# The second block's second product by seven products for two pairs of token chunks instead of one

## Chip, cores and metric

One core of a Trainium2 chip runs the whole program. The metric is the device time of one execution in microseconds, as the median of three runs.

## The reference

Attention (a coarse one on means of four tokens plus a local one in a band of seven), then two blocks on 2304 tokens of 512 channels. The change touches the second block and the layer norm ahead of it. Cut to that:

```python
def _moe2_ref(x, g_ln, w_ch1, w_ch2):          # x: (4, 576, 512), float32
    mu = np.mean(x, axis=-1, keepdims=True)
    var = np.mean((x - mu) ** 2, axis=-1, keepdims=True)
    xn = (x - mu) / np.sqrt(var + 1e-06) * g_ln
    ch = np.maximum(xn @ w_ch1, 0.0) @ w_ch2    # w_ch1: 512 x 2048, w_ch2: 2048 x 512, float64 in memory
    return (x + ch).astype(np.float32)
```

## The kernel before

Every instruction but the preparations is recorded with `add(engine, cost, prio, fn, r=, w=)`: its engine or a choice of engines, a cost, a priority, what it reads and writes. `Plan.order` (lines 137 to 240) then makes the order of the work by list scheduling on these costs: of the operations that are ready it takes the one that can begin first, and of those that can begin at the same time the one with the lowest priority number. Each engine then runs its own list in that order. All DMAs are issued by one engine, SP, one after the other; an SP instruction that waits holds all DMAs behind it. Buffers come from tags with a fixed number of slots, and a buffer takes a slot when the slot's former one has been read for the last time.

Every product is in split precision: each factor is a high and a low part (`F32R`), and `mm3` (lines 791 to 794) makes three matmuls for one, high by high, high by low, low by high.

The tokens are cut into six chunks of C = 384 (three tiles of 128). The first block works chunk by chunk. The second block, from about 384 us on, works on pairs of chunks: p = 0, 1 and 2, called here the first, the middle and the last pair. With two chunks and two halves of the channels, a product is a 2 by 2 product of blocks, which a Strassen-like scheme makes with seven block products in place of eight.

In each pair, `m2_prep` loads the pair's rows (x1t), makes the layer norm, writes it to `z_dram` and reads it back in a layout from which DVE can transpose (zb, lines 1009 to 1017: 32 DMAs per pair in runs of 32 floats), multiplies by g_ln and makes differences. `m2_split` makes the seven combinations xn in high and low parts. The first product takes for each f of eight (a block of 128 columns in each half of the 2048) seven products of six matmuls of 384 columns, with the weights `sa` loaded from `s_dram`, where `w1_combine` has put their seven combinations.

The second product has two forms. For p below KEEP (line 1163), `m2_h` splits each of the four results of an f into high and low parts, and `m2_acc` multiplies them with W2 as it is: 512 columns, six token tiles, two halves. For p from KEEP on, `m2_h_keep` leaves all results q in SBUF (in the slots that W2 had), and `m2_out_keep` makes seven products again: for each product and f a combination of q is split into hh and hl and multiplied with `ta`, loaded from `t_dram`, 256 columns, three token tiles. The combinations in `t_dram` are made by `w2_combine` from W2, through tiles `raw` and `t` (tag "wa", four slots), during the pair before the first one that needs them. PRM["keep"] is 1, so KEEP is 2: the first and the middle pair have the first form, the last pair the second, and w2_combine runs in the middle pair.

The weights `sa` have seven slots, one for each product; `ta` runs through eleven slots, these seven and the four of "wa". In the first product for f = 0 and 1 all results go to the two banks of the tag "pk"; later ones have more.

W2 is loaded as float64 and converted on ACT and DVE (`load_split`, `load_f32`): four of sixteen tiles in the last chunk of the first block, twelve during the first pair.

Of the kernel before, what the change touches and what calls it, by code (L numbers as in the profile page):

```python
# [9 lines left out]
F32 = mybir.dt.float32  # L10
# [26 lines left out]
    tp=0.5, tps=0.05, keep=1, tg=-2, ne=12, we=52.842, wes=25.704, wel=6.378,  # L37
# [37 lines left out]
class Plan:  # L75
# [61 lines left out]
    def order(self):  # L137
# [27 lines left out]
        while ready:  # L165
# [114 lines left out]
def attn_moe_kernel(  # L280
# [634 lines left out]

    def w1_convert(fo, d, prio):
        w1_early.add((fo, d))
        f = Buf(wk, [P, 512], F32, "wf", 2)
        load_f32(w_ch1[d * P:(d + 1) * P, 512 * fo:512 * fo + 512], f, prio)
# [4 lines left out]
    def w1_combine(g, j, prio):  # L924
# [3 lines left out]
        for x, fo, d in w1_parts(g, j):  # L928
# [4 lines left out]
            else:  # L933
                load_f32(w_ch1[d * P:(d + 1) * P, 512 * fo:512 * fo + 512], a[x], prio)
# [32 lines left out]
    def m2_prep(p, load_prio, prio):  # L967
# [39 lines left out]
        for j in range(2):  # L1007
            b = Buf(xpool, [P, 6, C], F32, "xT", 2, f"raw{j}")
            for q, (kt, c) in enumerate(((j, 2 * p), (j, 2 * p + 1), (j + 2, 2 * p), (j + 2, 2 * p + 1))):
                zb = Buf(wk, [P, C], F32, "tmu", 2, "zb")  # L1010
                for a in range(4):
                    add("SP", c_dma(32 * C * 4, 128), prio, lambda kt=kt, a=a, zb=zb, c=c: nc.sync.dma_start(
                        out=zb()[32 * a:32 * a + 32].rearrange("p (n f) -> p n f", f=32),
                        in_=z_dram[c * C:c * C + C, P * kt + 32 * a:P * kt + 32 * a + 32].rearrange(
                            "(n p) f -> p n f", p=32)), r=[(zd, (c, t)) for t in range(TT)], w=[(zb, a)], lat=2.2)
                add("DVE", c_dve(C), prio, lambda b=b, q=q, zb=zb: nc.vector.transpose(out=b()[:, q], in_=zb()),
                    r=[zb], w=[(b, q)])
                add("ACT", c_act(C, ap=1), prio, lambda b=b, q=q, kt=kt: nc.scalar.mul(
                    b()[:, q], b()[:, q], gln[:, kt:kt + 1]), r=[glb], w=[(b, q)])
# [4 lines left out]
            raws.append((b, s))  # L1024
# [3 lines left out]
    HL = "hl"  # L1028

    def b_place(p, i, j, x):  # L1030
        if p == 1 and i == 1:
            return w1tiles, f"alt{2 * j + x}", None
        if p == 1 and i == 6:
# [129 lines left out]
    KEEP = 3 - PRM["keep"]  # L1163

    def w2_combine(f, prio, after):
# [10 lines left out]
        raw = [Buf(w1tiles, [P, 512], F32, f"alt{2 * (f % 2) + k}", 1, "t") if KEEP == 1 else  # L1176
# [358 lines left out]
```

## Time and profile before

| | us |
|---|---|
| median of three runs | 765.13 (764.07 to 766.21) |
| the profiled execution | 766.57 |
| its span, first to last instruction | 764.8 |
| PE busy | 747.9 (98%) |
| DVE busy | 583.0 (76%) |
| ACT busy | 437.9 (57%) |
| POOL busy | 85.9 (11%) |

The span is the time from the first to the last instruction of the profiled execution; its own time is 1.8 us longer. A busy time is the time in which at least one instruction of the engine ran. PE is TensorE, DVE VectorE, ACT ScalarE, POOL GpSimd, SP the engine that issues the DMAs. Matmuls overlap: one of 384 columns is listed with some 0.34 us but the next begins 0.174 us after it, so a matmul's price is read from the distance of starts or from counts in a full stretch.

### The profile page before, as it was taken

To read this page: it belongs to the slowest core of one execution; us is meant where nothing else is said; L and a number is where in the kernel's file an instruction comes from. 1 tells how busy PE (TensorE), PEld (TensorE's weight loads), DVE (VectorE), ACT (ScalarE), POOL (GpSimd) and SP (SyncE) were. 2 spreads that over 40 slices of the span, in tenths; PEclk is the share of its full clock that TensorE was granted. 3 is DMA by queue.
4 is the path that set the end of the run, shared out by engine and by line. 5 is a ranking of instruction groups with operands and counts; after the bars stand their busy time and mean duration, and the time that the engine had idled before them with its cause. 6 is when DMAs were issued, how large, how long until landed. Compare 5 with 4: busy or idle time off the path is not lost.

```text
span 764.8 us, 16744 instructions
## 1 busy us (share of the span) xinstructions
PE 747.9 (98%) x6032; PEld 655.5 (86%) x6032; DVE 583.0 (76%) x1217; ACT 437.9 (57%) x1009; POOL 85.9 (11%) x140
## 2 busy tenths in 40 slices
PE   9999999999999999999999999999999999999998
PEld 6878777788778798888988899889887989999997
DVE  5899999998975958978989864476765776334986
ACT  5889998887785756858844541221332343343552
POOL 3011123112100000000110000020121110110101
PEclk9999999999999999999999999999999999999999
DMA  9998596877787896984778894469899986988784
GB/s 194 199 187 188 175 177 135 178 165 151 201 182 217 264 318 182 271 255 133 151 250 299 238 258 122 115 220 312 240 262 318 370 291 223 307 254 254 246 267 142
DMA packets 222623, 170.34 MB, mean 223 GB/s; under 512 B 129088, under 2 KB 168908, under 8 KB 222540
## 3 DMA queue, kind: packets, MB, share of 16 engines
q1 hardware_dynamic: 222540, 169.27, 78.6%
q8 instruction: 48, 0.79, 0.5%
q14 instruction: 35, 0.29, 0.1%
HBM read 122.56 MB, written 46.66 MB: 221 GB/s over the span
## 4 chain that ended last, share of the span: by engine, by line
PE 72%; DVE 13%; DMA 7%; ACT 4%; issue 2%; SPq 1%; POOL 0%; DVEq 0%; ACTq 0%; POOLq 0%
PE pso L793 7%; PE pso L794 7%; PE pso L792 7%; PE psh L792 7%; PE psh L793 6%; PE psh L794 6%; PE psk L792 4%; PE psv L792 4%; PE psk L794 3%; PE psk L793 3%; PE psv L793 3%; PE psv L794 3%; PE warm L447 2%; DMA w<-in_moe_w_ch_dram 2%; DMA zb<-z_dram 2%
## 5 line engine op out<-in xcount | busy, mean ns | idle before, releaser
L792 PE MATMUL psh<-xn,sa 128*128 128x384 f32 x336 | 114.1, 340 | 3.2 <-DVE c11l L1098 1.2
L793 PE MATMUL psh<-xn,sa 128*128 128x384 f32 x336 | 113.4, 338 | 0.0
L794 PE MATMUL psh<-xn,sa 128*128 128x384 f32 x336 | 113.1, 337 | 0.0
L792 PEld LDWEIGHTS psh<-xn,sa 128*128 128x128 f32 x336 | 63.1, 188 | 10.8 <-DVE c L1129 1.9
L793 PEld LDWEIGHTS psh<-xn,sa 128*128 128x128 f32 x336 | 63.1, 188 | 4.2 <-DVE xn L1066 0.2
L794 PEld LDWEIGHTS psh<-xn,sa 128*128 128x128 f32 x336 | 63.1, 188 | 0.0
L794 PE MATMUL pso<-ta,hl 128*128 128x256 f32 x168 | 47.4, 282 | 0.0
L793 PE MATMUL pso<-ta,hh 128*128 128x256 f32 x168 | 47.3, 281 | 0.0
L792 PE MATMUL pso<-ta,hh 128*128 128x256 f32 x168 | 47.1, 281 | 0.0
L389 ACT CAST hh<-q 128x384 fp32r<-128x384 f32 x55 | 28.4, 516 | 26.1 <-PE pso L793 23.9
L409 ACT ACTIVATE wf<-w 128x512 f32<-128x512 f32 x48 | 32.2, 671 | 14.8 <-DMA w<-in_moe_w_ch_dram 7.0
L416 DVE SCALAR_TENSOR_TENSOR wf<-wf,w 128x512 uint32<-128x512 uint32 x48 | 32.8, 686 | 8.9 <-ACT w L411 8.7
L393 ACT ACTIVATE kr<-psk 128x384 f32<-128x384 f32 x46 | 22.5, 489 | 24.2 <-PE psk L794 20.2
L857 DVE TENSOR_TENSOR kl<-kr,kh 128x384 fp32r<-128x384 f32 x43 | 23.8, 553 | 14.9 <-ACT kr L856 14.6
L411 ACT ACTIVATE w<-w 128x512 uint32<-128x512 uint8 x52 | 34.8, 669 | 0.0
L816 DVE SCALAR_TENSOR_TENSOR tmu<-xT,oms,tmu 128x384 f32<-128x384 f32 (+1 forms) x64 | 31.7, 512 | 2.1 <-ACT tmu L810 2.0
L420 DVE SCALAR_TENSOR_TENSOR wf<-w,wf 128x512 uint32<-128x512 uint32 x48 | 32.9, 686 | 0.3
L901 DVE TENSOR_TENSOR hl<-q,hh 128x384 fp32r<-128x384 f32 x47 | 26.0, 557 | 8.1 <-ACT hh L389 7.6
L794 PEld LDWEIGHTS pso<-ta,hl 128*128 128x128 f32 x168 | 31.7, 189 | 0.0
L792 PEld LDWEIGHTS pso<-ta,hh 128*128 128x128 f32 x168 | 31.7, 188 | 0.0
L793 PEld LDWEIGHTS pso<-ta,hh 128*128 128x128 f32 x168 | 31.6, 188 | 0.0
L810 ACT ACTIVATE tmu<-xT,vecs 128x384 f32<-128x384 f32 (+1 forms) x51 | 26.8, 538 | 6.9 <-DVE xrl L820 4.0
(573 smaller groups left out, 2178.5 us busy)
## 6 DMA issues: line engine op xcount, KB each, us to landing
sa<-s_dram SPq DMA_DIRECT2D x168, 256.0 KB, 3.7
w<-in_moe_w_ch_dram SPq DMA_DIRECT2D x32, 512.0 KB, 6.3
s_dram<-s SPq DMA_DIRECT2D x56, 256.0 KB, 4.0
ta<-t_dram SPq DMA_DIRECT2D x56, 256.0 KB, 3.1
t_dram<-t SPq DMA_DIRECT2D x32, 256.0 KB, 4.9
vw<-in_v_dram SPq DMA_DIRECT2D x62, 96.0 KB, 4.1
x_dram<-r SPq DMA_DIRECT2D x18, 256.0 KB, 3.3
x1t<-x_dram SPq DMA_DIRECT2D x6, 768.0 KB
```

What stands on the lines that cost most here:

```text
L389: return [("ACT", c_act(n), lambda: nc.scalar.copy(dst(), src()), False), ("DVE", c_dve(n, True), lambda: nc.vector.tensor_copy(dst(), src ...
L409: add("ACT", c_act(512), prio, lambda: nc.scalar.activation(f(), w64().bitcast(F32)[:, :, 1], AF.Abs, scale=2.0 ** -112), r=[w64], w=[f])
L411: add("ACT", c_act(512), prio, lambda: nc.scalar.activation(w64()[:, :, 0], w64().bitcast(U8).rearrange("p a (b c) -> p a b c", c=4)[:, :, ...
L416: lambda: nc.vector.scalar_tensor_tensor(fu(), fu(), 3, w64()[:, :, 0], op0=ALU.logical_shift_left, op1=ALU.bitwise_or),
L420: lambda: nc.vector.scalar_tensor_tensor(fu(), w64()[:, :, 1], 0x80000000, fu(), op0=ALU.bitwise_and, op1=ALU.bitwise_or),
L792: nc.tensor.matmul(ps, lh, rh, start=start, stop=False, skip_group_check=more)
L793: nc.tensor.matmul(ps, lh, rl, start=False, stop=False, skip_group_check=more)
L794: nc.tensor.matmul(ps, ll, rh, start=False, stop=stop, skip_group_check=more)
L810: add([("ACT", c_act(n, ap=1), lambda t=t, o=o, n=n, cur=cur, kt=kt: nc.scalar.mul(t()[:, o:o + n], cur(), mu[:, kt:kt + 1]), False), ("DV ...
L816: lambda t=t, o=o, n=n, prv=prv, kt=kt: nc.vector.scalar_tensor_tensor(t()[:, o:o + n], prv(), om[:, kt:kt + 1], t()[:, o:o + n], op0=ALU. ...
L857: add(either(C, lambda e: e.tensor_tensor(kl(), kr(), kh().bitcast(F32), op=ALU.subtract)), 0, prio, None, r=[kr, kh], w=[kl])
L901: add(either(n, lambda e: e.tensor_tensor(lo(), src(), hi().bitcast(F32), op=ALU.subtract)), 0, prio, None, r=r + wh, w=wl)
```

## The change

The middle pair's second product takes the second form too (keep = 2, so KEEP = 1). So `w2_combine` runs in the first pair, its operations waiting for the first pair's `m2_acc` three steps back instead of two (tg). Its tile `raw` moves to the tag "wf". For f below 6 the piece of W2 that the product i = 1 needs isn't written to `t_dram` but copied to SBUF by `w2_stay`, into the slots "xrh" and "xrl", and stays there for both pairs; so the last pair's xn of i = 1 and 6 take the places that the middle pair's have. In the pairs of the second form, `sa` and `ta` go through one ring of eleven slots. zb is read in runs of 128 floats (512 bytes) in 16 DMAs per pair, each for half a chunk and all four channel blocks, and transposed with a stride; for that the channels are permuted, which the loads of w_ch1 and g_ln follow. The planner gets a term that holds SP back after 330 us of planned time when transfers are behind.

```diff
-    tp=0.5, tps=0.05, keep=1, tg=-2, ne=12, we=52.842, wes=25.704, wel=6.378,
+    late=330.0, ahead=1.0, tp=0.5, tps=0.05, keep=2, tg=-3, b11=6, ne=12, we=52.842, wes=25.704, wel=6.378,
...
                 moved = max(moved, free[eng]) + cost
+                if at > PRM["late"]:
+                    free[eng] = max(free[eng], moved - PRM["ahead"])
                 end = moved + o.lat
...
+    def w1_rows(d, fo):
+        return w_ch1.rearrange("(p k) f -> k p f", k=KT)[d, :, 512 * fo:512 * fo + 512]
...
-            for q, (kt, c) in enumerate(((j, 2 * p), (j, 2 * p + 1), (j + 2, 2 * p), (j + 2, 2 * p + 1))):
-                zb = Buf(wk, [P, C], F32, "tmu", 2, "zb")
+            raws.append(b)
+        for c in (2 * p, 2 * p + 1):
+            for h in range(2):
+                zb = Buf(wk, [P, C // 64, P], F32, "w64", 2, "zb")
                 for a in range(4):
...
+                    row = c * C + C // 2 * h
+                    add("SP", c_dma(32 * C * 8, 512), prio, lambda a=a, zb=zb, row=row: nc.sync.dma_start(
+                        out=zb()[32 * a:32 * a + 32], in_=z_dram[row:row + C // 2, P * a:P * a + P].rearrange(
+                            "(n p) f -> p n f", p=32)), r=[(zd, (c, t)) for t in (range(2) if h == 0 else range(1, TT))],
+                        w=[(zb, a)], lat=2.2)
+                for kt in range(KT):
+                    b, q = raws[kt % 2], 2 * (kt // 2) + c % 2
+                    add("DVE", c_dve(C // 2), prio, lambda b=b, q=q, kt=kt, h=h, zb=zb: nc.vector.transpose(
+                        out=b()[:, q, C // 2 * h:C // 2 * h + C // 2], in_=zb()[:, :, kt:P:KT]),
+                        r=[zb], w=[(b, (q, h))])
...
+    KEEP = 3 - PRM["keep"]
+    N11 = PRM["b11"] if KEEP == 1 else 0
 
     def b_place(p, i, j, x):
-        if p == 1 and i == 1:
+        if (p == 1 or p == 2 and N11) and i == 1:
             return w1tiles, f"alt{2 * j + x}", None
-        if p == 1 and i == 6:
+        if (p == 1 or p == 2 and N11) and i == 6:
             return wp, f"s{16 + j}{HL[x]}", None
...
-    def m2_product(f, i, ps, xn, prio, first):
-
-        s = Buf(w1tiles, [P, 2, 2, P], F32R, f"sa{i}", 1)
+    def m2_product(f, i, ps, xn, prio, first, kept=False):
+
+        s = ring([P, 2, 2, P], "sa") if kept else Buf(w1tiles, [P, 2, 2, P], F32R, f"sa{i}", 1)
...
+    B11, stay = {}, [None]
+    n_ring = [0]
+
+    def ring(shape, name):
+        k = n_ring[0] % 11
+        n_ring[0] += 1
+        return Buf(w1tiles, shape, F32R, *((f"sa{SEQ[k]}", 1) if k < 7 else ("wa", 4)), name)
+
+    def w2_stay(f, prio):
+
+        if f % 3 == 0:
+            stay[0] = Buf(wk, [P, 3, 2, 256], F32R, f"xr{HL[f // 3]}", 1, "b11")
+        b = stay[0]
+        B11[f] = [View(b, (f % 3, x), lambda t, x=x: t[:, f % 3, x]) for x in range(2)]
+        for x in range(2):
+            add(copy(256, B11[f][x], lambda x=x: W2[f][x]()[:, :256]), 0, prio, None, r=[W2[f][x]], w=[B11[f][x]])
...
             for k, (i0, n) in enumerate(((0, 1), (1, 2))):
+                if k == 0 and f < N11:
+                    continue
...
-        raw = [Buf(w1tiles, [P, 512], F32, f"alt{2 * (f % 2) + k}", 1, "t") if KEEP == 1 else
+        raw = [Buf(wk, [P, 512], F32, "wf", 2, "t") if KEEP == 1 else
...
-                k = (F4 * n + f) % 11 if n < 6 or last else 0
-                ta = Buf(w1tiles, [P, 2, 256], F32R, *((f"sa{SEQ[k - 4]}", 1) if k > 3 else ("wa", 4)), "ta")
...
+                if i == 1 and f in B11:
+                    rh, rl = B11[f]
+                    need_ = [rh, rl]
+                else:
+                    ta = ring([P, 2, 256], "ta")
...
+            for f in range(N11):
+                w2_stay(f, T - 5 + f)
```

In `m2_h_keep` all seven calls of `m2_product` get the argument kept = True, and the load of g_ln reads "(p k) -> k p".

## Rows read from the trace of the kernel before

**Rows 1.** The page, busy time by engine: us, share of span, instructions.

```profile
PE 747.9 (98%) x6032; PEld 655.5 (86%) x6032; DVE 583.0 (76%) x1217; ACT 437.9 (57%) x1009; POOL 85.9 (11%) x140
```

**Rows 2.** Busy time by stage: stretch, length, engines (instructions), clock, DMA share, GB/s.

```profile
384.00:508.50 124.50, 123.40 (x611) 109.91 (x611) 84.41 (x167) 46.17 (x92) 10.90 (x9) 1.00 0.69 208
508.50:637.00 128.50, 126.39 (x624) 112.31 (x623) 93.30 (x198) 41.50 (x95) 18.34 (x21) 1.00 0.92 297
...
645.00:701.00 56.00, 56.00 (x316) 55.02 (x316) 21.85 (x39) 19.57 (x40) 5.10 (x5) 1.00 0.85 275
701.00:761.00 60.00, 59.99 (x506) 59.78 (x504) 52.34 (x107) 27.57 (x57) 6.62 (x6) 1.00 0.72 225
```

**Rows 3.** PE's waits, 570 to 645 us: line, releaser, us in total, times, longest.

```profile
PE psh L792 <- DVE c11l L1098: 1.2, 1, 1.2
PE psh L792 <- DVE c L1129: 0.7, 1, 0.7
PE psh L792 <- ACT u L385: 0.2, 1, 0.2
```

**Rows 4.** DVE in order of time near 577 us: start, length, instruction, idle before.

```profile
577.23 0.58 DVE L1016 STREAM_TRANSPOSE raw<-zb 128x384 f32<-128x384 f32 x1 [2.10 <-DMA zb<-z_dram]
```

**Rows 5.** PE in order of time at the end of the first pair.

```profile
507.32 0.40 PE L792 MATMUL pso<-w27h,c12h 128*128 128x512 f32 x1
...
508.72 0.34 PE L792 MATMUL psh<-xn,sa 128*128 128x384 f32 x1
```

**Rows 6.** Groups of DVE's instructions, 701 to 761 us: busy, mean ns, idle before.

```profile
L901 DVE TENSOR_TENSOR hl<-q,hh 128x384 fp32r<-128x384 f32 x46 | 25.5, 557 | 6.7 <-ACT hh L389 6.1
L905 DVE TENSOR_TENSOR q<-q,q 128x384 f32<-128x384 f32 x30 | 17.1, 578 | 0.0
```

**Rows 7.** The same, 384 to 508 us.

```profile
L1066 DVE TENSOR_TENSOR xn<-raw,xn 128x384 fp32r<-128x384 f32 x13 | 8.0, 622 | 1.9 <-ACT xn L389 1.8
```

**Rows 8.** DVE and POOL in order of time, 750 to 761 us.

```profile
752.99 1.27 DVE L1267 TENSOR_TENSOR uv<-uv 128x256 f32<-128x256 f32 x1
758.61 0.42 DVE L1267 TENSOR_TENSOR uv<-uv 128x256 f32<-128x256 f32 x1
752.96 3.33 POOL L901 TENSOR_TENSOR hl<-q,hh 128x384 fp32r<-128x384 f32 x3 [7.47 <-ACT hh L389]
```

**Rows 9.** PE in order of time at the start of the first pair.

```profile
386.78 0.39 PE L794 MATMUL psv<-wv7h,kl 128*128 128x512 f32 x1
...
389.66 0.45 PE L792 MATMUL psh<-xn,sa 128*128 128x384 f32 x1 [0.18 <-DVE u L1112]
```

**Rows 10.** Groups of DVE's instructions, 508 to 645 us; the additions L1180 by one.

```profile
L901 DVE TENSOR_TENSOR t<-t 128x256 fp32r<-128x256 f32 x25 | 10.7, 428 | 9.7 <-ACT t L389 9.6
L905 DVE TENSOR_TENSOR t<-t 128x256 f32<-128x256 f32 x21 | 8.8, 420 | 1.6 <-POOL t L905 1.3
...
L1180 DVE TENSOR_TENSOR t<-w210h,w210l 128x512 f32<-128x512 f32 x1 | 0.7, 693 | 0.1
```

**Rows 11.** The page, DMA issues: count, KB each, median us to landing.

```profile
sa<-s_dram SPq DMA_DIRECT2D x168, 256.0 KB, 3.7
...
ta<-t_dram SPq DMA_DIRECT2D x56, 256.0 KB, 3.1
...
zb<-z_dram SPq DMA_DIRECT2D x96, 48.0 KB, 3.0
```

**Rows 12.** DMA packets, MB and share of 16 engines: 510 to 570, then 570 to 645 us.

```profile
DMA packets 20290, 16.58 MB, mean 276 GB/s; under 512 B 12126, under 2 KB 13662, under 8 KB 20285
q1 hardware_dynamic: 20285, 16.52, 90.9%
DMA packets 16339, 22.72 MB, mean 303 GB/s; under 512 B 3071, under 2 KB 7679, under 8 KB 16332
q1 hardware_dynamic: 16332, 22.64, 89.0%
```

**Rows 13.** SP's issue of g_ln (ns), and of kin in order of time.

```profile
L1369 SPq DMA_DIRECT2D vraw<-in_moe_g_ln_dram x1: 293/293/293, 8.6 to 8.6; - x1
13.21 3.58 SPq L506 DMA_DIRECT2D kin<-in_k_dram  x4
```

More of the change, by code (lines that the diff above doesn't have):

```diff
@@ L918, in w1_convert @@
         f = Buf(wk, [P, 512], F32, "wf", 2)
-        load_f32(w_ch1[d * P:(d + 1) * P, 512 * fo:512 * fo + 512], f, prio)
+        load_f32(w1_rows(d, fo), f, prio)
         add("SP", c_dma(P * 2048), prio, lambda: nc.sync.dma_start(out=w1_dram[fo, d], in_=f()),
@@ L933, in w1_combine @@
             else:
-                load_f32(w_ch1[d * P:(d + 1) * P, 512 * fo:512 * fo + 512], a[x], prio)
+                load_f32(w1_rows(d, fo), a[x], prio)
         def put(i, src):
@@ L1008, in m2_prep @@
             b = Buf(xpool, [P, 6, C], F32, "xT", 2, f"raw{j}")
-            for q, (kt, c) in enumerate(((j, 2 * p), (j, 2 * p + 1), (j + 2, 2 * p), (j + 2, 2 * p + 1))):
-                zb = Buf(wk, [P, C], F32, "tmu", 2, "zb")
+            raws.append(b)
+        for c in (2 * p, 2 * p + 1):
+            for h in range(2):
+                zb = Buf(wk, [P, C // 64, P], F32, "w64", 2, "zb")
                 for a in range(4):
[L1012 to L1017, printed above, removed]
+                    row = c * C + C // 2 * h
[8 more added lines that the diff above has]
+                        r=[zb], w=[(b, (q, h))])
+        for j in range(2):
+            b = raws[j]
+            for q in range(4):
+                kt = j + 2 * (q // 2)
                 add("ACT", c_act(C, ap=1), prio, lambda b=b, q=q, kt=kt: nc.scalar.mul(
-                    b()[:, q], b()[:, q], gln[:, kt:kt + 1]), r=[glb], w=[(b, q)])
+                    b()[:, q], b()[:, q], gln[:, kt:kt + 1]), r=[glb, (b, (q, 0)), (b, (q, 1))], w=[(b, q)])
             s = lambda q, b=b: (lambda: b()[:, q])
@@ L1023, in m2_prep @@
             minus(C, s(5), s(3), s(1), prio, [(b, 3), (b, 1)], [(b, 5)])
-            raws.append((b, s))
+            raws[j] = b, s
         return raws
     HL = "hl"
+    KEEP = 3 - PRM["keep"]
+    N11 = PRM["b11"] if KEEP == 1 else 0
     def b_place(p, i, j, x):
-        if p == 1 and i == 1:
+        if (p == 1 or p == 2 and N11) and i == 1:
             return w1tiles, f"alt{2 * j + x}", None
-        if p == 1 and i == 6:
+        if (p == 1 or p == 2 and N11) and i == 6:
             return wp, f"s{16 + j}{HL[x]}", None
@@ L1162, in attn_moe_kernel @@
     acc_op = {}
-    KEEP = 3 - PRM["keep"]
+    B11, stay = {}, [None]
[11 more added lines that the diff above has]
+            add(copy(256, B11[f][x], lambda x=x: W2[f][x]()[:, :256]), 0, prio, None, r=[W2[f][x]], w=[B11[f][x]])
     def w2_combine(f, prio, after):
@@ L1309, in m2_out_keep @@
                 split(C, hh, hl, src, prio, [src], [hh], [hl])
-                k = (F4 * n + f) % 11 if n < 6 or last else 0
-                ta = Buf(w1tiles, [P, 2, 256], F32R, *((f"sa{SEQ[k - 4]}", 1) if k > 3 else ("wa", 4)), "ta")
-                add("SP", c_dma(P * 2048), prio - PRM["sld"], lambda ta=ta, f=f, i=i: nc.sync.dma_start(
-                    out=ta().bitcast(F32), in_=t_dram[f, TI[i]]),
-                    r=[(td, (TI[i], f, y)) for y in range(2)], w=[ta], lat=2.2)
-                rh, rl = (View(ta, None, lambda t, y=y: t[:, y]) for y in range(2))
-                need_ = [ta]
+                if i == 1 and f in B11:
[3 more added lines that the diff above has]
+                    ta = ring([P, 2, 256], "ta")
+                    add("SP", c_dma(P * 2048), prio - PRM["sld"], lambda ta=ta, f=f, i=i: nc.sync.dma_start(
+                        out=ta().bitcast(F32), in_=t_dram[f, TI[i]]),
+                        r=[(td, (TI[i], f, y)) for y in range(2)], w=[ta], lat=2.2)
+                    rh, rl = (View(ta, None, lambda t, y=y: t[:, y]) for y in range(2))
+                    need_ = [ta]
                 def mm(ts, f=f, hh=hh, hl=hl, rh=rh, rl=rl, cur=cur, fresh=fresh):
@@ L1369, in attn_moe_kernel @@
                 add("SP", 0.05, PRM["mu"], lambda i=i, src=src: nc.sync.dma_start(
-                    out=raw()[KT * i:KT * i + KT, :P], in_=src.rearrange("(k p) -> k p", p=P)), w=[(raw, i)], lat=2.2)
+                    out=raw()[KT * i:KT * i + KT, :P],
+                    in_=src.rearrange("(p k) -> k p" if src is g_ln else "(k p) -> k p", p=P)), w=[(raw, i)], lat=2.2)
             vps = Buf(ps_k, [P, 512], F32, "pk", 2, "vps")
```

14 lines of the change are left out of this document (7 added, 7 removed).

## The prediction

> **What bounds the kernel now.** I read the page first: PE is busy 98% of the span [rows 1], so time falls only if PE gets less to do or waits less. Then a table of busy time by stage, cut where the pairs of the second block begin and end [rows 2]. The reader is to see that from 384 us on PE is full in every stage (123.40 of 124.5, 126.39 of 128.5, 56.0 of 56.0, 59.99 of 60.0) at a granted clock of 1.00, that DVE is second (84.41, 93.30, 21.85, 52.34 us), and that the DMA share is highest in the middle pair, 0.92 at 297 GB/s. The middle pair's 128.5 us hold 2.1 us in which PE did nothing. Next the list of PE's waits in the second half of that pair [rows 3]: 1.2 + 0.7 + 0.2 = 2.1 us, all on DVE or ACT. The longest goes back to DVE's order of work: it stood 2.10 us before a transpose whose zb had not landed, and c11l, which PE wanted, was queued behind it [rows 4]. So PE bounds, and the DMA queue reaches PE through DVE.
>
> **The change part by part.** *Second product of the middle pair.* Now: 8 f by 6 token tiles by 2 halves by 3 = 288 matmuls of 512 columns. Six of them in a row begin from 507.32 until one of 384 columns begins at 508.72, so one takes 1.40 / 6 = 0.2333 us [rows 5]; 288 x 0.2333 = 67.2 us. After: 7 products by 8 f by 3 tiles by 3 = 504 of 256 columns. The last pair runs this form already: 506 matmuls in 59.99 us, 0.1186 each [rows 2]; 504 x 0.1186 = 59.8 us. All of it is on PE, and PE sets the end: **-7.4 us**. The first product, 336 matmuls of 384 columns at 56.0 / 316 = 0.177 us [rows 2], is the same in either form.
>
> *What DVE pays.* The old form's splits of c11 to c21 go (four per f), 32 q additions stay, and the out phase brings 56 subtractions hl of 0.557 us and 32 of q or pool of 0.578 us [rows 6], plus the additions into res. In the last pair this fits: DVE 52.34 and POOL 6.62 us beside 59.99 us of PE, without a wait [rows 2]. The middle pair's out phase gets something the last one has not: the split of the next pair's xn, 14 subtractions of 0.622 us [rows 7] and two more minus of 0.578, 9.9 us. 52.34 + 6.62 + 9.9 = 68.9 us against 59.8 us of PE, if DVE and POOL can't work at once: 9.1 us too much. That they hardly can, a row shows: while POOL did three hl (752.96 to 756.29), DVE's uv<-uv took 1.27 us, and 0.42 us when POOL was idle [rows 8]. Cost: 0 to +9.1 us. I take 0, since only the first two of seven xn are needed when the last pair begins, the rest up to 6 us later, and the stage after has DVE at 21.85 of 56.0 us [rows 2].
>
> The Trainium skill (SBUF — State Buffer, Who interferes with whom) says that a DVE instruction with two SBUF inputs and a GpSimd instruction that reads SBUF exclude each other for the whole instruction. The trace agrees as far as the 1.27 us goes. By that rule the out phase would be the 68.9 us, and this is the second rival below.
>
> *Hand-over to the last pair.* Before, its first steps ran between the middle pair's last 36 matmuls of 512 columns. After, nothing of that kind is left over, and steps f = 0 and 1 have two PSUM banks in the pool "pk", each waiting for an ACT or DVE instruction. The start of the first pair shows the price: between 386.78 and 389.66, 2.88 us, stand one 512-column matmul (0.23) and nine of 384 columns (0.177 each, 1.59), so 1.06 us was lost in one step [rows 9]. Two steps: 0 to 2.1 us; I take **+1.1**, since products of the out phase can fill in.
>
> *w2_combine moved by one pair.* Per f it adds two tiles of 512, makes four minus and four splits of 256, and writes 1 MB of t plus raw pieces of W2: 8 x 1792 KB = 14.7 MB, less 6 x 256 KB that are kept in SBUF, 13.1 MB. It leaves the middle pair, where the 2.1 us of waits stood, and enters the first, where it is queued on DVE, ACT and SP between the W2 loads and the sa loads. On DVE it took 10.7 + 8.8 us and sixteen additions of 0.69, 30.5 us in all [rows 10], so DVE in the first pair goes from 84.41 to some 115 of 124.5 us; the tile wf serves loads and combine in turn, and res of n = 0 and 3 after them. None of its output is wanted before the middle pair's out phase, 60 us later. So only its company costs: I move the 2.1 us with it, **0**, with -2.1 (they vanish) and +2.1 (both pairs have them) as ends.
>
> *Bytes.* One sa or ta is 256 KB [rows 11]. First pair after: 208 GB/s x 124.5 us = 25.9 MB, plus 13.1 = 39.0 MB, 313 GB/s. Middle pair after: 297 x 128.5 = 38.2 MB, less 14.7, plus 50 ta (13.1) = 36.6 MB in 119 us (128.5 - 7.4 - 2.1), 308 GB/s. Is there room? Two windows with different mixtures give the price of a packet [rows 12]: 12,126 short packets and 15.03 MB of long ones took 90.9% of 16 x 60 us, 3,071 and 22.33 MB 89.0% of 16 x 75 us; solved, 0.0153 us per 128-byte packet and 45.7 engine-us per MB, 350 GB/s at a full share. The zb loads are now 32 per pair of 384 packets [rows 11], 188 engine-us; after, 16 of 192 packets of 512 bytes, between 72 (by bytes) and 188 (four times a short one). With that the first pair comes to 111 to 119 of 124.5 us, the middle to 104 to 112 of 119 us, at most 95% and 94%. The middle pair ran at 92% with 2.1 us lost, so I take 0 here; the other end is the last rival.
>
> *Ring of 11, waits and queues.* Weights of the first product wait for 11 slots instead of their own one of seven; SP, in which sa waits for PE now, gets 11 x 1.06 = 11.7 us of lead (six matmuls of 0.177 each) against 7 x 1.06 = 7.4. Behind a waiting sa stand all other DMAs, as before. Cost 0. The 12 copies of w2_stay (256 columns, ACT, 0.4 us each) run while PE finishes the first pair's last step: 0, and if the cover is gone 12 x 0.4 = 4.8 us on ACT, half idle there.
>
> *zb in halves* makes 16 transposes of 192 instead of 8 of 384 per pair and SP issues 16 instead of 32: 0. *w_ch1 rows* keep their run length: 0. *g_ln* becomes 512 runs of 4 bytes; its row is 0.293 us of SP, and the nearest with as many packets, kin in four pieces of 576, takes 3.58 / 4 = 0.90 us [rows 13]: 0 to +0.6 early in the queue, I take **+0.3**. *The planner's new term* changes only the order on SP after its own 330 us: 0.
>
> **Sum.** -7.4 + 1.1 + 0.3 = -6.0 us. Against the profiled execution's 766.57 us (764.8 span and 1.8 around it): 760.6. That execution stood 1.44 us above the median of 765.13, so 759.1 us.
>
> **The rivals.** *All cover holds:* also the 2.1 us vanish, since zb costs fewer packets and the combine has left the pair with the most bytes, and the hand-over is free. 766.57 - 7.4 - 2.1 - 1.44 = 755.6. For it: the last pair lost nothing at all. Against: two pairs at a DMA share near 0.9 where there was one.
>
> *DVE and POOL become the bound* of the middle pair's out phase: 759.1 - 1.1 + 9.1 = 767.1, no change. For it: 1.27 against 0.42 us [rows 8]. Against: the free DVE time after it [rows 2].
>
> *Slower, the single DMA queue.* All transfers go through SP's queue in order, and the two pairs need 75.6 MB in what was 253 us. If the queue carries no more than the middle pair's 297 GB/s, they take 254.5 us: +1.5, with the hand-over and g_ln +2.9, so 768.0; at the 276 GB/s of 510 to 570 us [rows 12] it would be 274 us and 788. It decides from about 298 GB/s downward. For it: the first pair goes from 208 to 313. Against: 303 GB/s in 570 to 645 at 89% [rows 12], with less than 2.2 us lost.
>
> That the change does nothing is excluded as far as a trace can: the same code runs in the last pair at the 0.1186 us used here.
>
> **How the numbers follow.** 0.3%, or 2.3 us, is about what a measurement of this kernel can tell from no change. Chances: forecast 0.55 (own range 756.8 to 763), all cover 0.18, DVE and POOL 0.15, DMA queue 0.12. Faster (below 762.8): nine tenths of the first, the second, and a tenth of the third, 0.69. Within: 0.17. Slower (above 767.4): 0.14. The range goes from 754.6 (one us below the second case) to 766.8, which leaves part of the third and the fourth out above.
>
> **What would show it.** Right: pso of the middle pair as 504 matmuls of 256 columns near 0.1186 us; its out phase near 60 us; t_dram writes before the middle pair; waits of PE below 4 us from 384 us on. Hand-over wrong: no gap, or over 2.1 us, in the last pair's first two steps. DVE rival: hl as the releaser of pso, DVE and POOL together at the whole out phase. DMA rival: sa or ta as releasers of PE. The prediction is wrong altogether if PE shows new waits of more than 7 us.

## The result and the profile after

| | before | after |
|---|---|---|
| median | 766.31 (764.07 to 767.24, 6 runs) | 770.26 (767.09 to 773.96, 6 runs) |
| ratio | | 1.0052, 95% interval 1.0029 to 1.0074 |
| the profiled execution, its span | 766.57, 764.8 | 770.0, 767.9 |

The changed kernel is slower by 0.5%. The forecast was 759.1 us, with 766.8 as its upper bound; it was built on a median of 765.13 us for the kernel before, which six runs put at 766.31. One run below (777.16 us, of the kernel with tg = -1 and raw in "wf") was in a slower state of the clock and is left out of that kernel's figures.

The page of the changed kernel, busy time by engine, answers to [rows 1]:

```profile
PE 744.3 (97%) x6248; PEld 662.6 (86%) x6248; DVE 622.6 (81%) x1322; ACT 469.2 (61%) x1079; POOL 93.7 (12%) x143
```

PE has less to do than before, 744.3 against 747.9 us, and the span is still longer. Busy time by stage of the changed kernel, columns as in [rows 2]. The first pair now ends near 520 us, the middle pair's out phase fills the third row, and the last two rows are the last pair:

```profile
388.50:520.00 131.50, 123.02 (x588) 107.24 (x586) 109.36 (x236) 57.08 (x128) 15.58 (x17) 0.97 0.88 290
520.00:590.00 70.00, 69.05 (x397) 67.02 (x398) 53.52 (x116) 31.16 (x67) 8.57 (x8) 1.00 0.98 339
590.00:646.00 56.00, 56.00 (x471) 56.00 (x469) 53.59 (x111) 28.66 (x61) 10.09 (x8) 1.00 0.80 238
646.00:701.00 55.00, 55.00 (x320) 55.00 (x319) 20.94 (x39) 21.15 (x43) 6.07 (x6) 1.00 0.92 309
701.00:761.00 60.00, 60.00 (x498) 60.00 (x497) 50.78 (x101) 28.40 (x59) 6.62 (x6) 1.00 0.66 208
```

From 590 us on PE is full. Of the 9.4 us in which PE did nothing from 388.5 us on, 131.5 - 123.0 = 8.5 lie in the first pair, where before it was 1.1 of 124.5, and the granted clock of that stage is 0.97 instead of 1.00. PE's waits from 384 to 646 us, in the columns of [rows 3]:

```profile
PE psh L794 <- DVE c L1142: 2.9, 2, 2.2
PE pso L796 <- DVE c21l L1115: 2.8, 1, 2.8
PE pso L796 <- DVE c12l L1115: 1.5, 2, 1.2
PE psh L794 <- DMA sa<-s_dram: 1.0, 2, 0.6
PE psh L794 <- ACT u L387: 0.6, 2, 0.3
PE psh L794 <- DVE c L1146: 0.5, 1, 0.5
```

They sum to 9.3 us; the same list of the kernel before sums to 3.1:

```profile
PE psh L792 <- DVE c11l L1098: 1.2, 1, 1.2
PE psh L792 <- DVE c L1129: 0.8, 2, 0.7
PE psh L792 <- ACT u L385: 0.5, 2, 0.3
PE psh L792 <- DVE c L1125: 0.4, 1, 0.4
PE psh L792 <- DVE u L1112: 0.2, 1, 0.2
```

The longest wait of the changed kernel can be followed back through three engines. ACT, DVE and PE of the changed kernel in order of time near 487 us (start, length, instruction, idle before it and what ended that):

```profile
487.06 0.41 ACT L391 CAST t<-t 128x256 fp32r<-128x256 f32 x1 [2.44 <-DMA t_dram<-t]
...
487.50 0.43 DVE L903 TENSOR_TENSOR t<-t 128x256 fp32r<-128x256 f32 x1 [2.16 <-ACT t L391]
487.84 0.42 DVE L907 TENSOR_TENSOR t<-t 128x256 f32<-128x256 f32 x1
488.18 0.55 DVE L1115 SCALAR_TENSOR_TENSOR c21l<-c,c21h 128x384 fp32r<-128x384 f32 x1
...
485.56 0.40 PE L795 MATMUL pso<-w213l,c21h 128*128 128x512 f32 x1
488.78 0.79 PE L796 MATMUL pso<-w213h,c21l 128*128 128x512 f32 x1 [2.83 <-DVE c21l L1115]
```

A cast of `w2_combine` writes a tile t in the tag "wa", whose four slots come free when a write to `t_dram` has landed. ACT stood 2.44 us for that; DVE's next instruction, a subtraction of the combine, stood 2.16 us for ACT; and the split c21l, which PE wanted, was queued behind it. The landing that ACT waited for fell into a stretch in which the DMA engines were full (a share of 1.06 at 405 GB/s from 486 to 488 us, in the next rows), so the DMA queue has a part in this wait, though PE's list names DVE.

The wait costs more than its length. PE's starts after it are 0.32 us apart for 384 columns and 0.43 for 512, where the same matmuls before the gap started 0.177 and 0.233 apart. The granted clock is the column before the DMA share, in windows of 2 us:

```profile
486.00:488.00 2.00, 0.00 (x0) 0.00 (x0) 0.50 (x2) 0.41 (x1) 0.00 (x0) 1.00 1.06 405
488.00:490.00 2.00, 1.22 (x3) 1.04 (x4) 2.00 (x6) 0.74 (x2) 0.89 (x1) 0.55 1.00 385
490.00:492.00 2.00, 2.00 (x7) 1.90 (x7) 2.00 (x6) 0.81 (x3) 0.00 (x0) 0.50 0.42 157
492.00:494.00 2.00, 2.00 (x6) 1.52 (x6) 1.44 (x3) 0.08 (x1) 1.16 (x2) 0.50 0.44 151
494.00:496.00 2.00, 2.00 (x10) 1.77 (x9) 0.00 (x0) 0.00 (x0) 1.03 (x2) 0.74 0.97 374
496.00:498.00 2.00, 2.00 (x13) 2.00 (x12) 1.16 (x3) 0.83 (x3) 0.00 (x0) 1.00 0.31 87
```

At 0.50, which is 1.2 of 2.4 GHz, ten matmuls of 512 columns and six of 384 took the 6.33 us from 488.78 to 495.11; at full clock they are 10 x 0.233 + 6 x 0.177 = 3.4 us. So 2.9 us went into the clock.

With that the two profiled executions can be balanced: -7.4 (the new form), +6.2 (waits, 9.3 - 3.1), +2.9 (clock), and +1.7 at the start of the block, since the last matmul of 512 columns ahead of the first pair (the mark, below), at 386.78 us in [rows 9], is now at 388.47. The sum is +3.4 us; measured 770.0 - 766.57 = +3.4 (their spans differ by 3.1). That it fits so closely is luck in part: the -7.4 is worked out from counts and distances, and the mark differs by more than 1.7 us even between kernels that load g_ln alike (see below).

### The profile page after: what moved, and what is told of

Its sections match the earlier page's. It is cut to its first block, busy times and chain, and to the rows that moved or that the text cites. A ratio compares the mean times of both kernels' runs of the same rounds, so it can differ in the third digit from the quotient of the medians.

```text
span 767.9 us, 17471 instructions
## 1 busy us (share of the span) xinstructions
PE 744.3 (97%) x6248; PEld 662.6 (86%) x6248; DVE 622.6 (81%) x1322; ACT 469.2 (61%) x1079; POOL 93.7 (12%) x143
## 4 chain that ended last, share of the span: by engine, by line
PE 70%; DVE 12%; DMA 10%; ACT 5%; issue 3%; POOL 1%; SPq 0%; DVEq 0%; ACTq 0%; POOLq 0%
PE pso L796 6%; PE pso L794 6%; PE pso L795 6%; PE psh L794 6%; PE psh L795 6%; PE psh L796 6%; DMA w<-in_moe_w_ch_dram 4%; PE psk L794 4%; PE psv L794 4%; PE psv L795 4%; PE psv L796 4%; PE psk L796 3%; PE psk L795 3%; DMA sa<-s_dram 2%; PE sc L645 2%
## 5 line engine op out<-in xcount | busy, mean ns | idle before, releaser
L391 ACT CAST hh<-q 128x384 fp32r<-128x384 f32 x109 | 56.2, 516 | 48.0 <-PE pso L795 43.7
L796 PE MATMUL pso<-ta,hl 128*128 128x256 f32 x300 | 84.4, 281 | 0.0
L794 PE MATMUL pso<-ta,hh 128*128 128x256 f32 x300 | 84.3, 281 | 0.0
L795 PE MATMUL pso<-ta,hh 128*128 128x256 f32 x300 | 84.3, 281 | 0.0
L903 DVE TENSOR_TENSOR hl<-q,hh 128x384 fp32r<-128x384 f32 x92 | 51.3, 564 | 9.2 <-ACT hh L391 8.5
L796 PEld LDWEIGHTS pso<-ta,hl 128*128 128x128 f32 x300 | 56.7, 189 | 0.0
L795 PEld LDWEIGHTS pso<-ta,hh 128*128 128x128 f32 x300 | 56.6, 189 | 0.0
L794 PEld LDWEIGHTS pso<-ta,hh 128*128 128x128 f32 x300 | 56.5, 188 | 0.0
L1273 ACT ACTIVATE q<-q 128x384 f32<-128x384 f32 x48 | 25.2, 525 | 45.3 <-DVE q L1263 26.3
L903 POOL TENSOR_TENSOR hl<-q,hh 128x384 fp32r<-128x384 f32 x20 | 21.3, 1072 | 144.3 <-ACT hh L391 144.2
L907 DVE TENSOR_TENSOR q<-q,q 128x384 f32<-128x384 f32 x60 | 35.1, 592 | 0.0
```

What stands on the lines that cost most here:

```text
L391: return [("ACT", c_act(n), lambda: nc.scalar.copy(dst(), src()), False), ("DVE", c_dve(n, True), lambda: nc.vector.tensor_copy(dst(), src ...
L794: nc.tensor.matmul(ps, lh, rh, start=start, stop=False, skip_group_check=more)
L795: nc.tensor.matmul(ps, lh, rl, start=False, stop=False, skip_group_check=more)
L796: nc.tensor.matmul(ps, ll, rh, start=False, stop=stop, skip_group_check=more)
L903: add(either(n, lambda e: e.tensor_tensor(lo(), src(), hi().bitcast(F32), op=ALU.subtract)), 0, prio, None, r=r + wh, w=wl)
L907: add(either(n, lambda e: e.tensor_tensor(out(), a(), b(), op=op)), 0, prio, None, r=r, w=w)
```

## The experiments

The theory, A in the texts below: the new form gives its 7.4 us, and `w2_combine`, moved into the first pair and crowded there into its last 57 us, takes them back. Each text names its rivals. All edits are made in the changed kernel, and all ratios are to the kernel before, measured on the same chip in the same session; from session to session its median went from 765.89 to 766.53 us.

**Without the combine.** `w2_combine` isn't called, and each `ta` is read from `s_dram` with the same bytes.

```diff
-                out=ta().bitcast(F32), in_=t_dram[f, TI[i]]),
-                r=[(td, (TI[i], f, y)) for y in range(2)], w=[ta], lat=2.2)
+                out=ta().bitcast(F32), in_=s_dram[f, TI[i]].rearrange("p a b c -> p a (b c)")),
+                r=[(sd, (SEQ[TI[i]], f // 4, y, z)) for y in range(2) for z in range(2)], w=[ta], lat=2.2)
...
-                w2_combine(f, T + DP * (PRM["tp"] - 1.0 + PRM["tps"] * f), acc_op[...])
+                pass
```

> The changed kernel with w2_combine left out: nothing is written to t_dram, and each ta loads 256 KB of s_dram instead, so the output isn't the reference's. The load traffic of the middle and the last pair stays. Theory A (the combine, pressed into 464 to 521 us of the first pair, makes PE's waits there and the drop of the clock): the waits on c12l, c21l and c between 460 and 520 us (some 6.5 us) and the half-clock stretch (3 us) go, and the time is 770.3 - 9.5 = about 761 us. Theory B (the waits come from the first pair's other work or from the DMA queue): PE waits stay above 4 us there and the time is 766 us or more.

Measured: 763.06 us (760.46 to 766.39, 10 runs), ratio 0.9965 (0.994 to 0.999). The combine is worth 770.26 - 763.06 = 7.2 us, as much as the new form brings. Where it stood, PE now waits for nothing (columns as in [rows 2]):

```profile
460.00:480.00 20.00, 20.00 (x101) 17.99 (x100) 17.22 (x30) 10.58 (x20) 0.00 (x0) 1.00 0.82 259
480.00:500.00 20.00, 20.00 (x101) 17.97 (x100) 6.90 (x17) 4.76 (x11) 0.00 (x0) 1.00 0.54 157
500.00:520.00 20.00, 20.00 (x102) 18.21 (x101) 14.88 (x31) 7.35 (x17) 5.25 (x4) 1.00 0.59 186
```

So the waits from 464 us on are the combine's. Its DVE and ACT work and its writes went together here, so this run doesn't tell the one from the other. PE's waits from 384 to 646 us still sum to 7.8 us, at other places, and the time is 2 us above A's 761: the rest of the way to the forecast had to be elsewhere.

**g_ln.** The start of the block was late by 1.7 us, and g_ln is the only load at the start of the program that changed. Here it is read in 512-byte runs again, as before.

```diff
-    in_=src.rearrange("(p k) -> k p" if src is g_ln else "(k p) -> k p", p=P)), ...
+    in_=src.rearrange("(k p) -> k p", p=P)), ...
```

> The changed kernel with g_ln loaded as four runs of 512 bytes again, all else in the same order; g_ln's values then meet the wrong channels, so the output isn't the reference's. Theory: 512 runs of 4 bytes hold up the vw, kin and qin loads behind them on SP's queue at 9 us, which shifts all that follows by 1.7 us (the last psv matmul of the first block began at 388.47 instead of 386.78). Then 768.6 us and that matmul near 386.8. Rival: the shift is of another origin or differs from run to run, and the time stays at 770.3.

Measured: 767.10 us (761.57 to 771.34, 10 runs), ratio 1.0004 (0.9974 to 1.0033), 3.2 us less than the changed kernel. SP's issues behind g_ln in the changed kernel, in order of time (compare [rows 13] for g_ln's own 0.293 us):

```profile
8.71 0.30 SPq L1407 DMA_DIRECT2D vraw<-in_moe_g_ln_dram  x1
9.05 3.42 SPq L531 DMA_DIRECT2D vw<-in_v_dram  x4
```

g_ln's issue costs what it did. The four loads of vw behind it took SP 3.42 us, in the kernel before 2.33 and in this run 2.24, and the loads of kin began at 15.50 us, there at 13.21 and here at 12.91. That a queue entry's price is paid by the entries behind it was not in my sum.

The trace of this run also prices the clock. Its second block is the changed kernel's, and of the ten runs it is the one with a granted clock of 1.00. From the mark (385.37 us) to the end of the span it took 374.3 us, the changed kernel 379.4, the kernel before 378.0. PE's waits from 384 to 646 us sum to 7.1 us; the one on c21l, and the stretch around it at full clock:

```profile
PE pso L796 <- DVE c21l L1115: 1.6, 1, 1.6
480.00:490.00 10.00, 8.37 (x41) 7.04 (x40) 8.13 (x19) 3.29 (x9) 3.10 (x4) 1.00 0.99 341
```

The 5.1 us to the changed kernel are 2.2 of waits and the 2.9 of clock found above. So with the combine where the change put it, and g_ln as before, the second block still gained 3.7 us as long as the clock held; the waits took 4.0 of the 7.4 us. In the nine other runs the clock was lower, at 0.993 to 0.998.

**Both taken away.** The first edit, and g_ln read in 128 runs of 16 bytes straight into its tile, in the order of the permuted channels:

```diff
-    out=raw()[KT * i:KT * i + KT, :P],
-    in_=src.rearrange("(p k) -> k p" if src is g_ln else "(k p) -> k p", p=P)), ...
+    out=gln if i == 2 else raw()[KT * i:KT * i + KT, :P],
+    in_=src.rearrange("(p k) -> p k" if i == 2 else "(k p) -> k p", p=P)), ...
...
```

> w2_combine left out, and ta read from s_dram with the same bytes, as in e1, so the output of the middle and last pair isn't the reference's; and g_ln in 128 runs of 16 bytes straight into its tile. This is the changed kernel without the two terms that the prediction undervalued. If the sum holds but for them (the -7.4 us of PE are there, the hand-over costs 0 and not 1.1, DVE and POOL bound nothing), it should run at 766.2 - 7.4 = 759, within 757 to 761, on the clock's good executions. Rival: g_ln's 2.4 us at the start are caught up later, and the mended kernel stays at e1's 763; or the gain of the new form is smaller than 7.4.

Measured: 760.95 us (758.69 to 764.94, 9 runs), ratio 0.9933 (0.9909 to 0.9958), at the upper edge of what was expected. PE's waits from 384 to 646 us still sum to 6.9 us. The largest stands in this kernel and in the one without the combine, and in no other:

```profile
PE psh L794 <- issue: 2.8, 1, 2.8
```

At 399 us PE stands 2.8 us before a matmul, for nothing that the profile names. DVE was busy all that time (2.00 and 1.93 of 2.00 us in the first rows of the last section), and its t<-psh,t of 0.55 us, after which PE may write that bank again, began at 398.23 us, so it ended 0.10 us before the matmul; that DVE's order was the releaser here too is likely and not shown. Without this wait the kernel would be at some 758 us (an estimate, 760.95 - 2.8), and -7.4 says 759. So the form's gain is nearly all there once the two terms are gone. But this kernel makes no combination at all, where the kernel before makes them in the middle pair: it bounds what the change could give, and no run here has the form, the combine and the whole gain.

**The rest of the change alone.** keep = 1 and tg = -2 as before, so the middle pair has its old form and the combine its old place; zb, the rings, w_ch1 and the planner's term stay new, g_ln in 16-byte runs.

> The changed kernel with keep = 1 and tg = -2 again, so the combine runs in the middle pair and only the last pair has seven products in its second product, and with g_ln in 128 runs of 16 bytes; the 512-byte rows, the ring and the planner's term stay. Theory: these parts alone cost or bring little, the first pair runs without the waits of the changed kernel, and the time is that of the kernel before, 766.5, or up to 2 us less since zb no longer holds DVE up at 577 us. Rival: the late W2 loads or the strided transposes alone bring the waits, and the time is 769 us or more.

Measured: 766.02 us (761.44 to 768.79, 10 runs), ratio 0.9991 (0.9962 to 1.0021). The other parts alone give nothing that can be measured (the interval allows -2.9 to +1.6 us).

**zb, w_ch1 and g_ln as before, the rest new.** zb again in 128-byte runs in the tag "tmu".

> The changed kernel with the rows undone: zb in runs of 128 bytes in its old tag tmu, w_ch1 and g_ln in their old order. Theory A1 (zb took the tag w64, in which the W2 loads wait their turn, so seven W2 loads moved from 395 to 434 us to 433 to 462 us and the combine behind them into 464 to 521): W2 loads run before 440 us again, the combine begins by 440, PE waits under 4 us in the first pair, no half-clock stretch; with 1.7 us from g_ln the time is about 760 us. Theory A2 (DVE has too much to do in the first pair wherever it stands): waits of 6 us or more stay and the time is 767 us or more.

Measured: 769.13 us (766.96 to 773.37, 10 runs), ratio 1.0047 (1.0024 to 1.007); I had expected 760, and this is the range of the rival A2. The tag does move the work: in the changed kernel zb takes a slot of "w64", where the loads of W2 wait their turn, and of the loads from 384 to 521 us all but the first start between 433 and 462 us; here they start between 397 and 450. The combine moved forward with them (t writes from 436.0 to 498.4 us instead of 464.1 to 520.3), but the waits are now on another releaser, 450 to 530 us:

```profile
PE psh L794 <- DMA sa<-s_dram: 5.1, 2, 3.2
PE psh L794 <- DVE t L1128: 1.6, 1, 1.6
```

With short packets and the combine in one pair the queue does reach PE. But waits of 3.1 to 4.6 us on sa also stand in four kernels below that have the 512-byte runs, so this run shows neither that these runs are needed nor that their tag is what hurt.

**The planner told that t lands late.** The landing of a t write, 4.4 us at the median in the trace, is planned as 6.0 instead of 2.2 us.

```diff
-    out=t_dram[f, n], in_=t().bitcast(F32)), r=[t], w=[(td, (n, f, x)) for x in range(2)], lat=2.2)
+    out=t_dram[f, n], in_=t().bitcast(F32)), r=[t], w=[(td, (n, f, x)) for x in range(2)], lat=6.0)
```

> The changed kernel with one number of the planner changed: it takes 6.0 us instead of 2.2 us for the landing of the combine's t writes (median in the trace 4.4). Theory C (ACT and DVE stand in order behind casts whose tile t still waits for its write to land, because the planner thought it landed sooner): ACT's waits for t_dram fall from 5.7 us to under 2, the 2.83 us wait for c21l and the clock drop go, and the time is about 764 us. If the crowding alone is the cause the time stays within 2 us of 770.

Measured: 784.20 us (782.18 to 786.96, 4 runs), ratio 1.0244 (1.0199 to 1.0289). The combine was stretched into the middle pair (t writes to 539.2 us), and the tile res, which shares "wf" with the combine's raw, came late there. PE's waits from 530 to 600 us:

```profile
PE psh L794 <- DMA sa<-s_dram: 9.3, 4, 3.8
PE psh L794 <- DVE res L1170: 5.0, 1, 5.0
```

It backfired: ACT's waits for t_dram fell from 5.7 to 2.2 us, nearly as hoped, and the time went the other way. It says nothing for or against A but this: "wf" now ties W2 loads, combine and res together.

**Raw in tiles of its own, combine early.** raw goes back to the slots "alt0" to "alt3", with g_ln in 16-byte runs.

```diff
-    raw = [Buf(wk, [P, 512], F32, "wf", 2, "t") if KEEP == 1 else
+    raw = [Buf(w1tiles, [P, 512], F32, f"alt{2 * (f % 2) + k}", 1, "t") if KEEP == 1 else
```

> The changed kernel with two edits: g_ln comes straight into its place in 128 runs of 16 bytes, and w2_combine's tile raw is in the tags alt0 to alt3 instead of wf. Then the combine needn't wait its turn among the W2 loads: its first t write stands behind the 27th sa load instead of the 43rd, its last behind the 49th instead of the 63rd. Theory A (crowding: 38 us of DVE work in 57 us made the waits on c12l, c21l, c): these waits fall under 3 us, no half-clock stretch, about 767 - 6 = 761 us. Theory B (the first pair has no room for the combine anywhere, on DVE or on the DMA queue): waits of 6 us or more elsewhere in the first pair, 766 us or more.

Measured: 769.09 us (764.45 to 773.73, 10 runs), ratio 1.0032 (1.0002 to 1.0063). That is the range of B. The t writes stand between the 27th and the 49th of the sa loads in SP's queue, over 72 us (422.9 to 494.9) and among the W2 loads, and PE's waits sum to 9.9 us over the two pairs. Freed from "wf" alone, the combine costs as much elsewhere.

**Raw in tiles of its own, combine spread.** The same, and tg = -1, which brings the t writes between the 27th and the 64th sa load.

```diff
-    ... keep=2, tg=-3, ...
+    ... keep=2, tg=-1, ...
```

> As the run before, with tg = -1: the combine of f = 5, 6, 7 waits for the products two steps later, so the t writes are spread from the 27th to the 64th sa load, about 78 us. Theory A: the thinner it is spread the fewer waits; 759 to 760 us. Theory B: as the run before, 766 us or more.

Measured: 762.01 us (760.35 to 769.62, 6 runs), ratio 0.9953 (0.991 to 0.9996). Since that interval is wide, the kernel was run once more, with the two that follow, in one session:

> The kernel of e7 once more, unchanged, with more rounds: its gain of 4.5 us (762.0 against 766.5) had an interval that reached almost to no change. If the spreading of the combine is what gives it, 760 to 764 again. If e7 was a favourable draw of executions, 764 to 768, like e6, e8 and e9.

Measured: 764.15 us (760.50 to 766.97, 12 runs), ratio 0.998 (0.996 to 0.9999), the kernel before at 765.89.

**Spread order, raw in "wf".** The same kernel but for raw, which is in "wf" as in the changed one.

> As e7 (tg=-1, g_ln in 128 runs of 16 bytes straight into its tile) but with the combine's raw pieces in the two slots of wf again, as in the changed kernel. In this order SP's t writes stand between the 44th and the 65th sa load, against the 27th to the 64th in e7. Theory A (the crowding of the combine into the last 57 us of the first pair, caused by the tile its raw pieces share with the W2 loads, is what costs): the combine stays crowded, waits of 3 to 8 us behind DVE's splits c21l and c12l return in the first pair, time 764 to 768, over e7's 762.0 by 2 to 6. Rival B (the order of the combine's own steps, tg, is the whole difference, whatever tile its raw pieces are in): as e7, 760 to 763.

Measured: 770.35 us (765.47 to 772.77, 11 runs), ratio 1.0066 (1.0046 to 1.0086). This is the cleanest pair of all: one tile tag apart, on one chip, 764.15 and 770.35. The issues of t_dram<-t show what the tag does; first the kernel with raw in "wf", then the one with raw in "alt" (its first run): durations in ns, first and last start, then who waited for the landing (us, times).

```profile
L1225 SPq DMA_DIRECT2D t_dram<-t x32: 319/383/1393, 463.2 to 519.2; - x32
...
  ACT t L391: 5.4, 4
```

```profile
L1225 SPq DMA_DIRECT2D t_dram<-t x32: 319/382/587, 420.7 to 510.9; - x32
...
  ACT t L391: 1.0, 1
```

The changed kernel's row is like the first (464.1 to 520.3, ACT waited 5.7 us in 5 places). 32 writes in 56 us through four slots, or in 90. The tag also changes which engine the planner takes: of the combine's 64 subtractions and splits of 256 columns POOL has 8 with raw in "wf" and 33 with raw in "alt". Busy time of both halves of the first pair, the changed kernel and then the spread one (second run), columns as in [rows 2]:

```profile
408.00:464.00 56.00, 54.64 (x267) 47.65 (x267) 43.51 (x91) 21.82 (x41) 1.02 (x1) 1.00 0.91 288
464.00:521.00 57.00, 50.22 (x230) 43.12 (x229) 49.21 (x107) 28.30 (x70) 13.06 (x14) 0.94 0.85 292
```

```profile
408.00:464.00 56.00, 54.17 (x261) 48.09 (x260) 47.95 (x92) 25.92 (x56) 18.21 (x21) 0.97 0.94 309
464.00:521.00 57.00, 55.64 (x272) 48.60 (x271) 47.30 (x94) 28.91 (x69) 16.70 (x18) 1.00 0.92 314
```

Crowded, DVE goes from 43.51 of 56 to 49.21 of 57 us and PE loses 6.8 us in the second half; spread, DVE and POOL are level and PE loses 1.4 there (these two differ in tg and g_ln too). So the place that its tiles give the combine is worth some 6 us in this order. Whether that is the width of the stretch, POOL's share or the order behind PE's splits, this pair doesn't tell.

**Another spread order, and more slots for t.** Once tg = 0 with raw in "alt" (writes from the 25th to the 63rd sa load); once the changed kernel's order with t in eight slots instead of four, and g_ln in 16-byte runs:

```diff
-    t = Buf(w1tiles, [P, 2, 256], F32R, "wa", 4, "t")
+    t = Buf(w1tiles, [P, 2, 256], F32R, *(("wa", 4) if n % 2 else (f"alt{2 * (f % 2) + (n - 4) // 2}", 1)), "t")
```

> As e7 with tg=0 instead of -1: the t writes stand between the 25th and the 63rd sa load, so the combine is spread as widely as in e7, in another order of its single steps. Theory A (spreading is what counts): 760 to 764, like e7. Rival (e7's one order happens to be good, the spread is not the cause): 765 to 769, like e6 and e8.

> The changed kernel with g_ln in 128 runs of 16 bytes and eight slots for w2_combine's tile t instead of four (every second one in alt0 to alt3); the combine stays crowded, from the 43rd to the 60th sa load. If the waits for landing t writes, with which ACT held up DVE and PE at 485 us, are the larger part of the loss: waits on c12l and c21l under 2 us, clock 1.000, about 762 us. If the crowding on DVE is: c at 517 us still waited for 2 us, and about 766 us.

Measured: 766.51 us (764.54 to 770.67, 12 runs), ratio 1.001 (0.9988 to 1.0033), and 765.66 us (762.92 to 770.52, 10 runs), ratio 0.9991 (0.9968 to 1.0014). The first is in the rival's range and not in A's, and 2.4 us behind tg = -1 in the same session, though its writes are spread the widest. The second has them as dense as any and is no slower. In it ACT's wait for the landing falls from 5.7 to 0.3 us; what PE waits for then is DVE's queue itself (c12l 3.2 us, c11l 1.0). Against the kernel with g_ln in 512-byte runs (767.10) the slots bring 1.4 us, which is not resolved.

All kernels of the new form with the combine in the first pair and g_ln not in 4-byte runs, but for the one with the old zb:

| raw, tg | t writes within, us | of 64 on POOL | median, us |
|---|---|---|---|
| "wf", -3 | 52 | 9 | 767.10 |
| "wf", -3, eight slots | 46 | 8 | 765.66 |
| "wf", -1 | 56 | 8 | 770.35 |
| "alt", -3 | 72 | 36 | 769.09 |
| "alt", -1 | 90 and 93 | 33 | 762.01 and 764.15 |
| "alt", 0 | 101 | 23 | 766.51 |

Neither the width nor POOL's share puts the times in order, and the tag is worth 6.2 us at tg = -1 and nothing, or -2.0, at tg = -3 (there between two sessions, with g_ln in 16- and 512-byte runs). So A holds as far as the combine's place and order cost up to 6 us; that spreading as such is the cure is not shown, and why one order is good stays open.

## Why the prediction was wrong

The direction was wrong. The part that the change is named after was right: the gain is where the prediction put it. What failed is the term of w2_combine, put at 0 because DVE had room on the average, and by a smaller amount that of g_ln. In the two profiled executions the sum goes from -6.0 to +3.4 by +9.1 (combine, 6.2 of waits and 2.9 of clock), +1.4 (start of the block) and -1.1 (hand-over).

*Second product, -7.4 us: right.* Groups of PE's instructions of the changed kernel, 590 to 646 us (busy, mean ns, idle before):

```profile
L794 PE MATMUL pso<-ta,hh 128*128 128x256 f32 x150 | 42.3, 282 | 0.0
L795 PE MATMUL pso<-ta,hh 128*128 128x256 f32 x150 | 42.1, 280 | 0.0
L796 PE MATMUL pso<-ta,hl 128*128 128x256 f32 x149 | 41.8, 281 | 0.0
```

With ten more of 256 columns on b and twelve of 384 they come to 459 x 0.1186 + 12 x 0.177 = 56.6 us, one per cent over the 56.0 of the stretch, so the price holds. The 760.95 us without the two bad terms fit it, but for the 2.8 us of "issue", with what was said there.

*DVE and POOL in the out phase, 0 to +9.1, taken 0: right, but not for the reason given.* 53.59 and 10.09 us beside a PE that is full. The Trainium skill (SBUF — State Buffer, Who interferes with whom) says that a DVE instruction with two SBUF inputs and a GpSimd instruction that reads SBUF exclude each other; the sum of 63.7 us in a stretch of 56.0 doesn't show it here, since an instruction that is held up counts as busy (the 1.27 us of [rows 8]), and no run decides it. Its price at PE is 0. The reason was that most of the xn can come later; they didn't: of the 14 subtractions four ran from 584.8 us on, before the out phase, and ten in it, the last ending at 632.8. DVE and POOL kept pace all the same.

*Hand-over, +1.1: 0.* There is no wait of PE after 600 us, so this term was too large.

*Bytes and the queue, 0: right for the changed kernel* as far as PE's own list goes, sa 1.0 us of waits; the landing of t at a DMA share of 1.06 is the queue's part in the combine's price. The rival's ceiling of 297 GB/s falls: 520 to 590 us ran at 339 with PE at 69.05 of 70. The price that I solved for, 350 GB/s at a full share, fits (339 at 0.98). How near the queue is, the waits on sa in the kernel with the old rows and in those with raw in "alt" show.

*w2_combine, 0 with ends of ±2.1: this step failed.* I found 115 of 124.5 us of DVE and took "so only its company costs". That is an average over the pair. The combine's tile raw waits in "wf" among the W2 loads, and these wait in "w64" behind zb: its first t write stands at 464.1 us, and at 420 to 423 where raw has tiles of its own. I had written that wf "serves loads and combine in turn" and priced nothing for it. DVE's part also grew, since POOL has 9 of the 64 subtractions and splits where it had 18: 36.6 us instead of the 30.5 counted on. The work of a pair then goes into its second half, each t write occupies one of four slots for 4.4 us, and ACT and DVE, which work in order, stand with PE's splits behind them. Measured: 6.2 us of waits and 2.9 of clock in the trace, and 7.2 us by leaving it out. That the combine in the first pair costs this is shown; which of its parts (DVE's order, the landings, the engine chosen) is argued from the trace, and one tile tag changed it by 6.2 us in one order and not in another.

*zb in halves, 0:* a transpose of 192 takes 0.492 us and one of 384 took 0.574; 16 of them keep DVE busy for 7.0 us, since neighbours overlap, where 8 took 4.6. That is 2.4 us of DVE more, alone not visible (766.02).

*g_ln, +0.3: this failed too,* by size. Two pairs give it: 3.2 us (770.26 and 767.10) and 2.1 us (763.06 and 760.95), each with an interval wider than itself. The mark of [rows 9] is at 388.5 to 389.3 us in the three kernels that read g_ln in 4-byte runs and from 384.2 to 388.9 in the eleven others, so 2 to 3 us is likely and not exact. The mark alone proves little: among the eleven it differs by 4.7 us, with two at 388.2 and 388.9.

*What would show it.* The prediction named "waits of PE below 4 us from 384 us on" as the sign that it is right, and they were 9.3. "New waits of more than 7 us" were to make it wrong altogether; they were 6.2, and only with the 2.9 of clock, for which the sign had no place, is it that case. The releasers are splits and not sa. None of the rivals had this mechanism.

A version better than both: raw in "alt0" to "alt3", tg = -1 and g_ln in 16-byte runs, 762.01 and 764.15 us in two sessions against 766.48 and 765.89, ratios 0.9953 and 0.998 with upper ends just below 1. In the profile of its first run what is left is mostly sa, at 4.2 of 6.5 us.

## What to carry to other kernels

Work that is moved "beside" a bound engine is priced at the place where its inputs and tiles let it run, not at the average of the stage: follow the tag of each tile it waits for and ask what else takes turns there, and which engine the planner then takes. Look at engines that work in order for what is queued behind a wait on a landing. And put short-run loads at the price of the queue behind them, not of their own issue.

## What the runs showed of the hardware

A gap of PE was dear in one place and not in another of the same length. After 2.83 us (up to 488.78 in the changed kernel) the granted clock was 0.50 for 6 us. After the 2.8 us of "issue" in the kernel without the combine and with g_ln mended it stayed at 1.00 (windows of 2 us there):

```profile
396.00:398.00 2.00, 0.09 (x1) 0.00 (x0) 2.00 (x5) 1.28 (x3) 0.00 (x0) 1.00 0.96 359
398.00:400.00 2.00, 1.12 (x6) 1.15 (x7) 1.93 (x5) 1.95 (x4) 0.00 (x0) 1.00 0.97 376
400.00:402.00 2.00, 2.00 (x13) 1.82 (x12) 2.00 (x5) 0.58 (x2) 0.00 (x0) 1.00 0.89 324
```

In the kernel with tg = -1 and raw in "wf", where PE stood 4.72 us, the clock was at 0.50 already inside the gap:

```profile
508.00:510.00 2.00, 0.00 (x0) 0.00 (x0) 2.00 (x7) 0.88 (x3) 0.00 (x0) 0.97 0.94 336
510.00:512.00 2.00, 0.00 (x0) 0.00 (x0) 2.00 (x6) 0.74 (x2) 0.00 (x0) 0.50 1.07 396
512.00:514.00 2.00, 1.42 (x4) 1.42 (x5) 2.00 (x6) 1.04 (x3) 0.00 (x0) 0.50 0.38 140
```

So the length of a gap alone doesn't tell whether it is paid twice. The Trainium skill (TensorE: Matmul & The Clock Gate, HAM oscillation — how this bites in real kernels) says that a wait of PE for data can bring the clock down, so that what follows starts slow. The gaps of 2.83 and 4.72 us agree; that it need not happen, the one of 2.8 us shows. The clock also spreads the times: of the ten runs of the kernel with g_ln in 512-byte runs the one with a granted clock of 1.00 took 761.57 us, the nine others, at 0.993 to 0.998, 764.33 to 771.34. Differences below some 2 us between these kernels are for that reason not resolved here.
